# Splitting three of seven second-layer products into seven once more, in an attention and gated feed-forward kernel

## The chip, the cores and the metric

The kernel runs on one core of one Trainium2 chip. The metric is the device time in microseconds (us) of one execution; the figure for a kernel is the median of its runs. A profile of one execution goes with it: what each engine did and when. PE is the matrix engine (TensorE), PEld its weight loads, DVE is VectorE, ACT is ScalarE, POOL is GpSimd, SP the engine whose queue starts most DMAs.

## The reference

Everything is float32. For 8 batches of 576 rows, attention without a softmax, normalised by its root mean square, gives x of 4608 tokens by 512 features. Then comes a gated feed-forward layer with 1536 hidden features.

```python
kv  = einsum('bhsd,bhse->bhde', k, v)
out = einsum('bhsd,bhde->bhse', q, kv)
rms = sqrt(mean(out * out, axis=-1, keepdims=True) + 1e-06)
x   = (out / rms * g_norm).transpose(0, 2, 1, 3).reshape(4608, 512)

gate = 1.0 / (1.0 + exp(-(x @ w_gate)))
val  = x @ w_val
return gate * val @ w_out            # (4608, 512)
```

## The kernel before

The tokens are worked off in nine groups of 512. Group 0 is computed plainly. Groups 1 to 8 use Strassen's scheme in Winograd's form: a product of two 2x2 block matrices is made of seven block products instead of eight, at the price of sums of blocks before and after. The first layer (x with `w_gate` and `w_val`) uses it, and its own small part a second time within one of its products. The second layer (`h @ w_out`, h being gate times value) uses it once. Each product of the second layer is six matmuls, one for each 128 hidden features, of 128 tokens by 256 output columns. It is done for two halves g of the tokens:

```python
def second_layer_fast(c):
    b = {(j, n): w2[...] ...}                      # four blocks of w_out
    for g in range(2):
        t1, t2 = slice(P * g, P * g + P), slice(GH + P * g, GH + P * g + P)
        (i_a, pa), (i_b, pb) = (take() for _ in range(2))     # PSUM banks
        def product(ps, hs, ws, new):
            for f in range(NF2):                               # 6
                nc.tensor.matmul(ps, hs(f), ws[:, f, :], start=(new and f == 0), stop=(f == NF2 - 1), ...)
                if f % 3 == 2:
                    slot()                                     # one step of other work

        product(pa, lambda f: gv[c, f][:, t1], b[1, 1], True)
        o2 = sg_tile()
        nc.scalar.copy(out=o2[:, d1], in_=pa)
        product(pb, lambda f: s12[c, f][:, t2], t2w[2], True)
        o1 = sg_tile()
        tt(out=o1[:, d2], in0=pb, in1=o2[:, d1], op=ALU.add)
        product(pa, lambda f: gv[c, f + NF2][:, t1], b[2, 1], False)
        nc.scalar.copy(out=o1[:, d1], in_=pa)
        product(pb, lambda f: gv[c, f][:, t2], t2w[3], False)
        tt(out=o2[:, d2], in0=pb, in1=o2[:, d1], op=ALU.add)
        ...
            product(pc, lambda f: s12[c, f][:, t1], t2w[1][:, :, x], True)
            tt(out=o2x, in0=pc, in1=o2x, op=ALU.add)
        product(pb, lambda f: gv[c, f + NF2][:, t2], t2w[4], False)
        tt(out=o2[:, d1], in0=pb, in1=o2[:, d1], op=ALU.add)
        store(c, 2 + g, o2)
        ...
            product(pc, lambda f: s4[c, f][:, t1], b[2, 2][:, :, x], False)
            tt(out=o1[:, y], in0=pc, in1=o1[:, y], op=ALU.add)
        store(c, g, o1)
        if g == 1:
            load_late(c + 2)                                   # k and v two groups on
```

`tt` is VectorE's `tensor_tensor`. `s12` and `s4` are sums of h, made on VectorE at the end of each step of the first layer (`h_sum`, `h_sums`, lines 847 to 856). `t2w[1..4]` are sums of blocks of `w_out`, made once. In the very last half the two products marked with `x` are cut into two halves of 128 columns (`parts`), so that the last output can leave sooner.

The first layer needs sums of x and of its weights. Those of x are made on VectorE, in steps that are put in the queue `fill`, of which each call of `slot()` does one; those of the weights on GpSimd:

```python
def x_sums(c):                                      # 4 of 128x512 and, in x_sums2, 4 of 128x128
    sx[c] = s = sums.tile([P, 3, NK, GH], FP32, tag="sx", name="sx", bufs=1)
    return [lambda: tt(out=s[:, 0], in0=a[2, 1], in1=a[2, 2], op=ALU.add), ...] + x_sums2(c, a[1, 2])

def w_sum(f, i):                                    # 128x256, L720
    nc.gpsimd.tensor_tensor(out=tw[f, i], in0=..., in1=..., op=ALU.subtract)

def w_sums2(f):                                     # four of 128x128, L713
    nc.gpsimd.tensor_tensor(out=tw2[i], in0=in0, in1=..., op=ALU.subtract)

for c in range(1, NG):
    if c + 1 < B:
        steps = feed(c + 1)                         # attention of the next batch, as steps for slot()
        ...
        spread(steps, ...)
    first_layer_fast(c)                             # its last part starts the weight sums of the next group
    sums_of(c + 1)                                  # x_sums of the next group
    second_layer_fast(c)
    flush()
```

There are five PSUM banks for products; `take()` takes the one that has been free longest, `give()` puts it back. Every engine works through its instructions in the order of the program.

Of the kernel before, what the change touches and what calls it, by code (L numbers as in the profile page):

```python
# [20 lines left out]
def kernel(  # L21
# [313 lines left out]
    def slot():  # L335
        if fill:
            fill.popleft()()
# [3 lines left out]
    def feed(b):  # L341
# [34 lines left out]
        def two_pairs(n0):  # L376


            d = {}
            ms = sb.tile([P, NQ, NJ], FP32, tag="ms2", name="ms2", bufs=1)  # L380
            sq = sqs[:, 0:2 * S].rearrange("p (r c) -> p r c", r=NQ)
            units = [slice(NJ // 2 * i, NJ // 2 * (i + 1)) for i in range(2)]

            def by_head(t):
                return t.rearrange("p r (n d) -> p r n d", d=HD)

            def u_mm():
                d["u"] = u = at_ps()[:, 0:NQ, 0:2 * QC]
                for which in range(2):
                    for g in range(JH):  # L390
                        for i in range(NC):
                            for r in range(NQ):
                                for e in range(2):
                                    c, o = NJ * HD * e + QC * i + PH * g, HD * (JH * which + g)
                                    nc.tensor.matmul(u[HD * e:HD * e + HD, r, o:o + HD],  # L395
                                                     qTs[QB * r:QB * r + QB, (n0 + which) % 2, c:c + PH],
                                                     kvq[QB * r:QB * r + QB, (n0 + which) % NHP, NC * e + i],
                                                     start=(i == 0), stop=(i == NC - 1))

            def u_square():  # L400
                nc.scalar.activation(out=sq, in_=d["u"], func=AF.Square)

            def u_sum(i):
                nc.vector.tensor_reduce(out=ms[:, :, units[i]], in_=by_head(sq)[:, :, units[i]], axis=AX.X, op=ALU.add)

            def u_root():
                nc.scalar.activation(out=ms, in_=ms, func=AF.Sqrt, bias=eps, scale=1.0 / HD)

            def u_norm(i):
                if i == 0:  # L410
                    nc.vector.reciprocal(ms, ms)
                m_ = ms[:, :, units[i]]
                nc.vector.tensor_tensor(out=by_head(sq)[:, :, units[i]], in0=by_head(d["u"])[:, :, units[i]],
                                        in1=m_.unsqueeze(3).to_broadcast([P, NQ, NJ // 2, HD]), op=ALU.mult)

            def x_turn(i):


                for which in range(2):
                    nc.vector.transpose(xTs[:, i, which],  # L420
                                        sq.rearrange("p r (w g i c) -> p w i r g c", w=2, g=JH, i=NC)[:, which, i])
                m = n0 % NHP
# [426 lines left out]
    def h_sums(c, f):  # L849
# [5 lines left out]
        tt(out=one[:, h2], in0=one[:, h1], in1=one[:, h2], op=ALU.subtract)  # L855
        tt(out=s4[c, f], in0=two[:, h1], in1=s[:, h2], op=ALU.subtract)

    def second_layer_fast(c):
        b = {(j, n): w2[:, NF2 * (j - 1):NF2 * j, DH * (n - 1):DH * n] for j in (1, 2) for n in (1, 2)}
        d1, d2 = slice(0, DH), slice(DH, DM)  # L860
        for g in range(2):
            t1, t2 = slice(P * g, P * g + P), slice(GH + P * g, GH + P * g + P)
            (i_a, pa), (i_b, pb) = (take() for _ in range(2))

            last = (c, g) == (NG - 1, 1)
            parts = [slice(0, DH // 2), slice(DH // 2, DH)] if last else [slice(0, DH)]

            def product(ps, hs, ws, new):
                for f in range(NF2):
                    nc.tensor.matmul(ps, hs(f), ws[:, f, :], start=(new and f == 0), stop=(f == NF2 - 1),  # L870
                                     skip_group_check=True)
                    if f % 3 == 2:
                        slot()

            product(pa, lambda f: gv[c, f][:, t1], b[1, 1], True)
            o2 = sg_tile()
            nc.scalar.copy(out=o2[:, d1], in_=pa)
            product(pb, lambda f: s12[c, f][:, t2], t2w[2], True)
            o1 = sg_tile()
            tt(out=o1[:, d2], in0=pb, in1=o2[:, d1], op=ALU.add)  # L880
            product(pa, lambda f: gv[c, f + NF2][:, t1], b[2, 1], False)
            nc.scalar.copy(out=o1[:, d1], in_=pa)
            if last:
                store(c, g, o1, d1)
            product(pb, lambda f: gv[c, f][:, t2], t2w[3], False)
            tt(out=o2[:, d2], in0=pb, in1=o2[:, d1], op=ALU.add)
            pcs = []
            for x in parts:
                i_c, pc = take()
                pc = pc[:, 0:x.stop - x.start]  # L890
                pcs.append((i_c, pc))
                product(pc, lambda f: s12[c, f][:, t1], t2w[1][:, :, x], True)
                o2x = o2[:, DH + x.start:DH + x.stop]
                tt(out=o2x, in0=pc, in1=o2x, op=ALU.add)
            product(pb, lambda f: gv[c, f + NF2][:, t2], t2w[4], False)
            tt(out=o2[:, d1], in0=pb, in1=o2[:, d1], op=ALU.add)
            store(c, 2 + g, o2)
            give(i_a)
            give(i_b)
            for (i_c, pc), x in zip(pcs, parts):  # L900
                give(i_c)
                product(pc, lambda f: s4[c, f][:, t1], b[2, 2][:, :, x], False)
                y = slice(DH + x.start, DH + x.stop)
                tt(out=o1[:, y], in0=pc, in1=o1[:, y], op=ALU.add)
                if last:
                    store(c, g, o1, y, (nc.sync, nc.scalar))
            if not last:
                store(c, g, o1)
            if g == 1:
                load_late(c + 2)  # L910

    def sums_of(c):
        if c < NG:
            fill.append(lambda: fill.extendleft(reversed(x_sums(c))))

    sums = ctx.enter_context(tc.tile_pool(name="sums", bufs=2, side="right"))
    for n in (1, 2, 3, 4):
        for f in (0, NF2):
            w_sum(f, n)
# [27 lines left out]
    for c in range(1, NG):  # L947
        if c + 1 < B:
            steps = feed(c + 1)
            if c == 1:  # L950

                i = 4
                while w2_sums:
                    steps.insert(i, (DVE, w2_sums.popleft()))
                    i += 3
            spread(steps, (1, 2, 3, 4, 5) if c == 1 else (2, 3, 4, 5))
        first_layer_fast(c)
        sums_of(c + 1)
        second_layer_fast(c)
        flush()  # L960

# [29 lines left out]
```

## Time and profile before

| | |
|---|---|
| time, median of 3 runs | 1077.0 us (1076.07 to 1077.27) |
| span in the profile | 1073.9 us |
| mean granted TensorE clock | 0.998 |
| second layer of one group without attention steps (group 7) | 921.50 to 957.76 us |
| second layer of a group with attention steps (group 4) | 582.09 to 620.42 us |
| additions of L855 (VectorE, 128x256), min / median / max | 409 / 943 / 950 ns |
| additions of L702 (VectorE, 128x128), min / median / max | 281 / 281 / 699 ns |
| sums of L713 with two original blocks (GpSimd, 128x128), min / median / max | 445 / 459 / 933 ns |

How to read it: "busy" is the time in which an engine has at least one instruction running. The records of PE overlap, so its pace is read from the distance of start times and not from the duration of one. A line of the timeline has the start and the length in us, the engine, the line of the source, the operation, what is written and read, the shape, how many alike are merged (x12), and in brackets the idle time before it with what ended it. A matmul of float32 shows as two records.

### The profile page before, as it was taken

Reading aid. Unit: us, or ns where it says so; the run is one execution under the profiler, and the core shown is the slowest. Engines: PE = TensorE matmul, PEld = TensorE weight load, DVE = VectorE, ACT = ScalarE, POOL = GpSimd, SP = SyncE. Lnnn points to the kernel's source line nnn. Section 1 sums busy time; section 2 is a strip of 40 time slices with the busy share of each in tenths; the row PEclk is TensorE's granted clock in tenths of the full one; section 3 lists DMA queues with packets and bytes.
Section 4 is the critical chain, followed back from the end, with each engine's and each line's share of the span. In section 5 each row is a group of like instructions: output and inputs, shape, how many; then the busy total and the mean of one; then the engine's idle time right before and its main releaser. Section 6 shows DMA issues by size and latency. Waiting matters only on the chain.

```text
span 1073.9 us, 19464 instructions
## 1 busy us (share of the span) xinstructions
PE 1062.2 (99%) x7514; PEld 882.4 (82%) x7514; DVE 712.0 (66%) x1461; ACT 309.0 (29%) x737; POOL 442.1 (41%) x630
## 2 busy tenths in 40 slices
PE   8999999999999999999999999999999999999997
PEld 7544448888888888888888888888888888888886
DVE  4897767894579547863778357945786388628841
ACT  4654323331243113320433134312431122112210
POOL 0000035880367216640666046713663077307800
PEclk9999999999999999999999999999999999999999
DMA  9944710002400141012301140014001200010001
GB/s 259 254 157 157 244 29 22 24 17 60 119 12 13 45 128 36 12 35 62 100 23 34 42 120 13 25 45 137 13 12 27 58 2 1 2 38 1 1 1 40
DMA packets 69115, 64.96 MB, mean 60 GB/s; under 512 B 23712, under 2 KB 63008, under 8 KB 69024
## 3 DMA queue, kind: packets, MB, share of 16 engines
q1 hardware_dynamic: 68768, 63.69, 21.1%
q8 instruction: 60, 0.98, 0.4%
q14 instruction: 31, 0.25, 0.1%
q10 hardware_dynamic: 256, 0.03, 0.1%
HBM read 47.19 MB, written 9.44 MB: 53 GB/s over the span
## 4 chain that ended last, share of the span: by engine, by line
PE 97%; DVE 1%; DMA 1%; SPq 0%; issue 0%; ACT 0%; DVEq 0%
PE mm L728 46%; PE mm L870 27%; PE mm L732 7%; PE mm L556 7%; PE mm L653 4%; PE at L395 2%; PE at L354 1%; PE at L556 1%; DMA q<-in_q_dram 1%; PE two L291 0%; PE two L261 0%; PE mm L634 0%; PE two L318 0%; PE two L272 0%; PE at L360 0%; SPq L97 0%
## 5 line engine op out<-in xcount | busy, mean ns | idle before, releaser
L720 POOL TENSOR_TENSOR tw<-gv 128x256 f32<-128x256 f32 x192 | 156.2, 823 | 232.1 <-DVE w L202 145.0
L728 PE MATMUL mm<-xT,tw 128*128 128x256 f32 x768 | 198.4, 381 | 0.0
L728 PE MATMUL mm<-sx,tw 128*128 128x256 f32 x768 | 197.4, 380 | 0.0
L802 POOL TENSOR_TENSOR sg<-sg 128x256 f32<-128x256 f32 x48 | 35.6, 742 | 341.1 <-ACT sg L801 340.9
L720 POOL TENSOR_TENSOR tw<-gv,tw 128x256 f32<-128x256 f32 x192 | 155.0, 828 | 0.0
L728 PEld LDWEIGHTS mm<-xT,tw 128*128 128x128 f32 x768 | 137.3, 190 | 17.5 <-issue 2.9
L728 PEld LDWEIGHTS mm<-sx,tw 128*128 128x128 f32 x768 | 134.9, 191 | 12.4
L773 DVE TENSOR_TENSOR gv<-gv,sg 128x256 f32<-128x256 f32 x192 | 108.7, 585 | 0.0
L728 PE MATMUL mm<-sx,gv 128*128 128x256 f32 x384 | 91.2, 380 | 0.0
L728 PE MATMUL mm<-xT,gv 128*128 128x256 f32 x384 | 90.8, 379 | 0.0
L870 PE MATMUL mm<-w,gv 128*128 128x256 f32 x384 | 89.1, 381 | 0.7 <-DVE gv L773 0.7
L870 PE MATMUL mm<-t2w,gv 128*128 128x256 f32 x384 | 88.7, 381 | 0.0
L870 PE MATMUL mm<-w,s 128*128 128x256 f32 (+1 forms) x408 | 88.3, 367 | 0.0
L764 ACT ACTIVATE sg<-sg 128x256 f32<-128x256 f32 x96 | 40.0, 416 | 151.0 <-DVE sg L763 150.9
L739 ACT COPY sg<-mm 128x256 f32<-128x256 f32 x96 | 35.8, 373 | 162.7 <-PE mm L728 160.9
L870 PEld LDWEIGHTS mm<-w,gv 128*128 128x128 f32 x384 | 72.5, 190 | 12.2 <-DVE gv L773 2.5
L870 PEld LDWEIGHTS mm<-w,s 128*128 128x128 f32 x408 | 74.1, 190 | 9.4
L728 PEld LDWEIGHTS mm<-xT,gv 128*128 128x128 f32 x384 | 72.9, 190 | 10.4 <-issue 0.5
L728 PEld LDWEIGHTS mm<-sx,gv 128*128 128x128 f32 x384 | 72.5, 190 | 10.0
L870 PEld LDWEIGHTS mm<-t2w,gv 128*128 128x128 f32 x384 | 72.4, 190 | 10.0
L556 PE MATMUL mm<-xT,gv 128*128 128x512 f32 x176 | 77.4, 594 | 0.0
L745 DVE TENSOR_TENSOR gv<-mm,sg 128x256 f32<-128x256 f32 x96 | 37.0, 413 | 41.2 <-PE mm L728 37.8
(120 smaller groups left out, 1548.4 us busy)
## 6 DMA issues: line engine op xcount, KB each, us to landing
q<-in_q_dram SPq DMA_DIRECT2D x24, 288.0 KB
st<-in_moe_w_gate_dram SPq DMA_DIRECT2D x12, 512.0 KB
st<-in_moe_w_val_dram SPq DMA_DIRECT2D x12, 512.0 KB
st<-in_moe_w_out_dram SPq DMA_DIRECT2D x12, 512.0 KB
kv<-in_k_dram SPq DMA_DIRECT2D x24, 256.0 KB
kv<-in_v_dram SPq DMA_DIRECT2D x24, 256.0 KB
out_dram<-sg SPq DMA_DIRECT2D x23, 192.0 KB
xT<-xTs SPq DMA_DIRECT2D x48, 72.0 KB
```

What stands on the lines that cost most here:

```text
L395: nc.tensor.matmul(u[HD * e:HD * e + HD, r, o:o + HD], qTs[QB * r:QB * r + QB, (n0 + which) % 2, c:c + PH], kvq[QB * r:QB * r + QB, (n0 + ...
L556: nc.tensor.matmul(self.ps[i], w[("wg", "wv")[i], self.f][:, m, :], xT[self.c][:, m, :], start=(m == 0), stop=(m == NMT - 1), skip_group_c ...
L653: nc.tensor.matmul(ps[t], gv[0, f][:, P * t:P * t + P], w["wo", f], start=(f == 0), stop=(f == NFT - 1), skip_group_check=True)
L720: nc.gpsimd.tensor_tensor(out=tw[f, i], in0=b[in0], in1=b[in1] if isinstance(in1, tuple) else tw[f, in1], op=ALU.subtract)
L728: nc.tensor.matmul(ps, wt[:, m, :], xs[:, m, :], start=(new and m == 0), stop=(m == NK - 1), skip_group_check=True)
L732: nc.tensor.matmul(ps, wt, xs, start=new, stop=True, skip_group_check=True)
L739: nc.scalar.copy(out=d["sg"][:, h2], in_=d["pa"])
L745: tt(out=d["h"][:, h1], in0=d["pb"], in1=d["sg"][:, h2], op=ALU.add)
L764: nc.scalar.activation(out=d["sg"][:, h2], in_=d["sg"][:, h2], func=AF.Sigmoid)
L773: tt(out=d["h"][:, h], in0=d["h"][:, h], in1=d["sg"][:, h], op=ALU.mult)
L802: nc.gpsimd.tensor_tensor(out=g2[:, h1], in0=g2[:, h1], in1=g2[:, h2], op=ALU.add)
L870: nc.tensor.matmul(ps, hs(f), ws[:, f, :], start=(new and f == 0), stop=(f == NF2 - 1), skip_group_check=True)
```

## The change

Three of the seven products of the second layer, those with `b[2, 1]`, `t2w[4]` and `b[2, 2]`, are each taken over both halves of the tokens at once and split into seven smaller products by the same scheme: small products are three matmuls of 128 tokens by 128 columns. Seven times three matmuls of 128 columns stand in place of twice six matmuls of 256 columns. This is meant to take an eighth of these products' columns from the matrix engine.

Each split needs four sums of weights and four of h, each of three tiles of 128x128. There is no free memory for them, so they are written to places that are no longer read: the sums of x (`sx`, now one fixed tile), and columns of `gv` (h) and `s12` whose products are done. As these places are used again, the sums of weights are made anew in each group. The three sets of weight sums and one set of h sums are made on GpSimd, two sets of h sums on VectorE. The sums of x for the next group come only after split 1, which reads `sx`. Steps of the attention end earlier (idle steps removed, the sums of `w_out` placed at every second step instead of every third).

```diff
-        return steps + two_pairs(n0 + 2) + [(PE, idle)] * 4
+        return steps + two_pairs(n0 + 2)
...
-        sx[c] = s = sums.tile([P, 3, NK, GH], FP32, tag="sx", name="sx", bufs=1)
+        sx[c] = s = sx_tile
...
+    def sums2(engine, x, out, weights):             # 4 sums, each over N3 = 3 tiles
+        ...
+                engine.tensor_tensor(out=o[i][j], in0=u0, in1=u1, op=...)
...
     def second_layer_fast(c):
+        spare = sx[c].rearrange("p a k (h t) -> p (a k h) t", h=2)
+        a4, a2, a3 = h_quarters(gv, hi, 2), h_quarters(gv, hi, 0), h_quarters(s4, lo, 0)
+        b4, b2, b3 = (w_quarters(x) for x in (t2w[4], b[2, 1], b[2, 2]))
+        t4 = sums2(nc.gpsimd, b4, thirds([spare[:, i] for i in range(4 * N3)]), True)
+        for g in pair:
+            product(pa[g], of(gv, lo, g), b[1, 1], True)
+            nc.scalar.copy(out=o2[g][:, d1], in_=pa[g])
+        t2 = sums2(nc.gpsimd, b2, thirds(of(gv, lo, 0) + of(gv, lo, 1)), True)
+        for g in pair:
+            product(pb[g], of(s12, lo, 2 + g), t2w[2], True)
+            nc.scalar.copy(out=o1[g][:, d1], in_=o2[g][:, d1])
+            tt(out=o1[g][:, d2], in0=pb[g], in1=o2[g][:, d1], op=ALU.add)
+        r2 = thirds(of(s12, lo, 2) + of(s12, lo, 3))
+        s4_ = sums2(nc.gpsimd, a4, r2[:3], False)
+        for g in pair:
+            product(pb[g], of(gv, lo, 2 + g), t2w[3], False)
+            tt(out=o2[g][:, d1], in0=pb[g], in1=o2[g][:, d1], op=ALU.add)
+        t3 = sums2(nc.gpsimd, b3, thirds(of(gv, lo, 2) + of(gv, lo, 3)), True)
+        for g in pair:
+            product(pc, of(s12, lo, g), t2w[1], True)
+            tt(out=o2[g][:, d2], in0=pc, in1=o2[g][:, d1], op=ALU.add)
+            tt(out=o1[g][:, d2], in0=pc, in1=o1[g][:, d2], op=ALU.add)
+        s2_ = sums2(nc.vector, a2, thirds(of(s12, lo, 0) + of(s12, lo, 1))[:3], False)
+
+        def split(o, x, a, sa, w_, tw_, done=None):
+            ...                                     # small(): 3 matmuls of 128 columns
+            small(pd, a[1, 1], w_[1, 1], True)
+            add(o[0][:, l], pd)
+            small(pf, a[1, 2], w_[2, 1], True)
+            add(o[0][:, l], pf)
+            slot()
+            small(pd, sa[2], tw_[2], False)         # goes on in the bank that add read
+            add(o[0][:, r], pd)
+            small(pe, sa[1], tw_[1], True)
+            add(o[1][:, r], pe)
+            slot()
+            small(pd, sa[3], tw_[3], False)
+            tt(out=y, in0=y, in1=pd.unsqueeze(1).to_broadcast([P, 2, P]), op=ALU.add)
+            small(ph, a[2, 2], tw_[4], True)
+            add(o[1][:, l], ph)
+            slot()
+            small(pe, sa[4], w_[2, 2], False)
+            add(o[0][:, r], pe)
+            slot()
+
+        split(o2, d1, a4, s4_, b4, t4)
+        for g in pair:
+            store(c, 2 + g, o2[g])
+        if not ends:
+            fill.extend(x_sums(c + 1))
+        s3_ = sums2(nc.vector, a3, r2[:3], False)
+        split(o1, d1, a2, s2_, b2, t2)
+        ...
+            split(o1, d2, a3, s3_, b3, t3)
+            for g in pair:
+                store(c, g, o1[g])
+        load_late(c + 2)
...
-                    i += 3
+                    i += 2
...
-        sums_of(c + 1)
```

More of the change, by code (lines that the diff above doesn't have):

```diff
@@ L856, in h_sums @@
         tt(out=s4[c, f], in0=two[:, h1], in1=s[:, h2], op=ALU.subtract)
+    N3 = NF2 // 2
+    d1, d2 = slice(0, DH), slice(DH, DM)
+    tok = [slice(P * i, P * i + P) for i in range(G // P)]
+    def sums2(engine, x, out, weights):
+        o = dict(zip((1, 2, 4, 3), out))
+        if weights:
+            ops = ((1, (1, 2), (1, 1)), (2, (2, 2), 1), (4, (2, 1), 2), (3, (2, 2), (1, 2)))
+        else:
+            o[3] = x[2, 1]
+            ops = ((1, (2, 1), (2, 2)), (2, 1, (1, 1)), (3, (1, 1), (2, 1)), (4, (1, 2), 2))
+        for i, in0, in1 in ops:
+            for j in range(N3):
+                u0, u1 = (x[n][j] if isinstance(n, tuple) else o[n][j] for n in (in0, in1))
+                engine.tensor_tensor(out=o[i][j], in0=u0, in1=u1,
+                                     op=ALU.add if i == 1 and not weights else ALU.subtract)
+        return o
@@ L858, in second_layer_fast @@
     def second_layer_fast(c):
         b = {(j, n): w2[:, NF2 * (j - 1):NF2 * j, DH * (n - 1):DH * n] for j in (1, 2) for n in (1, 2)}
[L860 to L870, printed above, removed]
-                                     skip_group_check=True)
[L872 to L910, printed above, removed]
@@ L912, in sums_of, with product @@
-    def sums_of(c):
-        if c < NG:
-            fill.append(lambda: fill.extendleft(reversed(x_sums(c))))
+        ends = c == NG - 1
+        pair = range(2)
+        lo, hi = range(NF2), range(NF2, NFT)
+        def product(ps, hs, ws, new):
+            for f in range(NF2):
+                nc.tensor.matmul(ps, hs[f], ws[:, f, :], start=(new and f == 0), stop=(f == NF2 - 1),
+                                 skip_group_check=True)
+                if f % N3 == N3 - 1:
+                    slot()
@@ new lines, in of, with thirds, h_quarters, w_quarters @@
+        def of(tiles, fs, t):
+            return [tiles[c, f][:, tok[t]] for f in fs]
+        def thirds(tiles):
+            return [tiles[i:i + N3] for i in range(0, len(tiles), N3)]
+        def h_quarters(tiles, fs, t):
+            return {(i, k): of(tiles, fs[N3 * (k - 1):N3 * k], t + i - 1) for i in (1, 2) for k in (1, 2)}
+        def w_quarters(ws):
+            return {(k, n): [ws[:, f, tok[n - 1]] for f in range(N3 * (k - 1), N3 * k)] for k in (1, 2) for n in (1, 2)}
+        spare = sx[c].rearrange("p a k (h t) -> p (a k h) t", h=2)
@@ new lines, in second_layer_fast @@
+        a4, a2, a3 = h_quarters(gv, hi, 2), h_quarters(gv, hi, 0), h_quarters(s4, lo, 0)
+        b4, b2, b3 = (w_quarters(x) for x in (t2w[4], b[2, 1], b[2, 2]))
+        t4 = sums2(nc.gpsimd, b4, thirds([spare[:, i] for i in range(4 * N3)]), True)
+        o2, o1, pa, pb = {}, {}, {}, {}
+        for g in pair:
+            i_, pa[g] = take()
+            product(pa[g], of(gv, lo, g), b[1, 1], True)
+            o2[g] = sg_tile()
+            nc.scalar.copy(out=o2[g][:, d1], in_=pa[g])
+            give(i_)
@@ new lines, in second_layer_fast @@
+        t2 = sums2(nc.gpsimd, b2, thirds(of(gv, lo, 0) + of(gv, lo, 1)), True)
+        i_b = {}
+        for g in pair:
+            i_b[g], pb[g] = take()
+            product(pb[g], of(s12, lo, 2 + g), t2w[2], True)
+            o1[g] = sg_tile()
+            nc.scalar.copy(out=o1[g][:, d1], in_=o2[g][:, d1])
[5 more added lines that the diff above has]
+            tt(out=o2[g][:, d1], in0=pb[g], in1=o2[g][:, d1], op=ALU.add)
+            give(i_b[g])
@@ new lines, in second_layer_fast, with small, add @@
+        t3 = sums2(nc.gpsimd, b3, thirds(of(gv, lo, 2) + of(gv, lo, 3)), True)
+        for g in pair:
+            i_, pc = take()
+            product(pc, of(s12, lo, g), t2w[1], True)
+            tt(out=o2[g][:, d2], in0=pc, in1=o2[g][:, d1], op=ALU.add)
+            tt(out=o1[g][:, d2], in0=pc, in1=o1[g][:, d2], op=ALU.add)
+            give(i_)
+        s2_ = sums2(nc.vector, a2, thirds(of(s12, lo, 0) + of(s12, lo, 1))[:3], False)
+        def split(o, x, a, sa, w_, tw_, done=None):
+            (i_d, pd), (i_e, pe), (i_f, pf), (i_h, ph) = (take() for _ in range(4))
+            pd, pe, pf, ph = (ps[:, 0:P] for ps in (pd, pe, pf, ph))
+            l, r = slice(x.start, x.start + P), slice(x.start + P, x.stop)
+            def small(ps, hs, ws, new):
+                for j in range(N3):
+                    nc.tensor.matmul(ps, hs[j], ws[j], start=(new and j == 0), stop=(j == N3 - 1),
+                                     skip_group_check=True)
+            def add(t, ps):
+                tt(out=t, in0=ps, in1=t, op=ALU.add)
+            small(pd, a[1, 1], w_[1, 1], True)
[9 more added lines that the diff above has]
+            small(pd, sa[3], tw_[3], False)
+            y = o[1][:, x].rearrange("p (n c) -> p n c", n=2)
+            tt(out=y, in0=y, in1=pd.unsqueeze(1).to_broadcast([P, 2, P]), op=ALU.add)
+            small(ph, a[2, 2], tw_[4], True)
+            add(o[1][:, l], ph)
+            slot()
+            if done:
+                done()
+            small(pe, sa[4], w_[2, 2], False)
+            add(o[0][:, r], pe)
+            slot()
+            for i in (i_d, i_f, i_h, i_e):
+                give(i)
@@ new lines, in second_layer_fast @@
+        split(o2, d1, a4, s4_, b4, t4)
[5 more added lines that the diff above has]
+        split(o1, d1, a2, s2_, b2, t2)
+        if ends:
+            for g in pair:
+                store(c, g, o1[g], d1)
+            l, r = slice(DH, DH + P), slice(DH + P, DM)
+            split(o1, d2, a3, s3_, b3, t3,
+                  lambda: [store(c, 1, o1[1], d2), store(c, 0, o1[0], l)])
+            store(c, 0, o1[0], r, (nc.sync, nc.scalar))
+        else:
+            split(o1, d2, a3, s3_, b3, t3)
+            for g in pair:
+                store(c, g, o1[g])
@@ L916 @@
+        load_late(c + 2)
     sums = ctx.enter_context(tc.tile_pool(name="sums", bufs=2, side="right"))
+    sx_tile = sums.tile([P, 3, NK, GH], FP32, name="sx", bufs=1)
     for n in (1, 2, 3, 4):
```

## The prediction

> **What bounds the kernel now.** I read the page's first lines, then the chain that ended last, then the matrix engine's order of time in one second layer.
>
> ```profile
> span 1073.9 us, 19464 instructions
> ...
> PE 1062.2 (99%) x7514; PEld 882.4 (82%) x7514; DVE 712.0 (66%) x1461; ACT 309.0 (29%) x737; POOL 442.1 (41%) x630
> ...
> PE 97%; DVE 1%; DMA 1%; SPq 0%; issue 0%; ACT 0%; DVEq 0%
> PE mm L728 46%; PE mm L870 27%; PE mm L732 7%; PE mm L556 7%; PE mm L653 4%; PE at L395 2%; PE at L354 1%; PE at L556 1%; DMA q<-in_q_dram 1%; PE two L291 0%; PE two L261 0%; PE mm L634 0%; PE two L318 0%; PE two L272 0%; PE at L360 0%; SPq L97 0%
> ```
>
> TensorE (PE) is busy for 99% and is 97% of the chain, so the kernel gains only if PE has less to stream, and loses whatever makes PE wait. The second layer (L870) is 27%. What a product costs there is read from start times, since neighbouring records overlap. This is the timeline of PE in the last group, where the old kernel already has two products cut into 128-column halves:
>
> ```profile
> 1055.20 2.75 PE L870 MATMUL mm<-t2w,gv 128*128 128x256 f32 x12
> 1057.79 2.84 PE L870 MATMUL mm<-w,s 128*128 128x128 f32 x24
> 1060.47 2.75 PE L870 MATMUL mm<-t2w,gv 128*128 128x256 f32 x12
> 1063.06 2.84 PE L870 MATMUL mm<-w,s 128*128 128x128 f32 x24
> ```
>
> Each fp32 matmul is two records. A product of six matmuls (x12) takes 1057.79 - 1055.20 = 2.59 us, 0.216 us a record of 256 columns. The 24 records of 128 columns take 1060.47 - 1057.79 = 2.68 us, 0.112 us each. So a half-width matmul is nearly half as dear, even with weights of its own each time.
>
> The other two engines matter because the change gives them its additions. First VectorE (DVE) in the group that starts its second layer at 921.50, then the same lines in the last group:
>
> ```profile
> 923.64 0.94 DVE L854 TENSOR_TENSOR s<-s,gv 128x256 f32<-128x256 f32 x1
> 924.51 0.94 DVE L855 TENSOR_TENSOR gv<-gv 128x256 f32<-128x256 f32 x1
> 925.38 0.94 DVE L856 TENSOR_TENSOR s<-gv,s 128x256 f32<-128x256 f32 x1
> ...
> 929.41 0.29 DVE L702 TENSOR_TENSOR sx<-sx,xT 128x128 f32<-128x128 f32 x1
> 929.62 0.28 DVE L703 TENSOR_TENSOR xT<-xT 128x128 f32<-128x128 f32 x1
> ...
> 1030.77 0.42 DVE L854 TENSOR_TENSOR s<-s,gv 128x256 f32<-128x256 f32 x1
> 1031.11 0.42 DVE L855 TENSOR_TENSOR gv<-gv 128x256 f32<-128x256 f32 x1
> ```
>
> and GpSimd (POOL) beside the first of them and after:
>
> ```profile
> 924.27 1.77 POOL L720 TENSOR_TENSOR tw<-gv,tw 128x256 f32<-128x256 f32 x2
> 963.04 0.73 POOL L802 TENSOR_TENSOR sg<-sg 128x256 f32<-128x256 f32 x1 [37.00 <-ACT sg L801]
> ...
> 968.31 0.46 POOL L713 TENSOR_TENSOR tx<-gv,gv 128x128 f32<-128x128 f32 x1
> ```
>
> A 256-column addition with both inputs in SBUF starts every 0.34 us on DVE when POOL is idle (1030.77 to 1031.11) and every 0.87 us when POOL works (923.64 to 924.51). A 128-column one starts every 0.21 us alone (929.41 to 929.62). POOL is idle from 926.0 to 963.0, the whole second layer but its first 4.5 us.
>
> **What the skill says.** The Trainium skill, "SBUF — State Buffer", section "Who interferes with whom": a VectorE instruction with two SBUF inputs contends with a GpSimd instruction that reads SBUF. The trace agrees: 0.34 us against 0.87 us above. "PSUM — Partial Sum Buffer", section "Engine vs sequencer instructions": ScalarE, VectorE and GpSimd queues are strict FIFO; an addition at the head of DVE's queue therefore holds back a later one that PE needs. The trace shows every engine in program order. "TensorE: Matmul & The Clock Gate", section "Step-by-step: what each phase is for": LDWEIGHTS are pulled ahead of running matmuls. It agrees: a weight load lasts 190 ns, yet 128-column records start every 112 ns. The same page, section "What's actually happening": after an idle window of about 3.4 us PE's clock is halved until it has been busy for about as long. No run here shows it; the granted clock was 0.998.
>
> **The change, part by part.** The second layer had 14 products per group of 512 tokens (seven for each half), 14 x 2.59 = 36.3 us. Now three of the seven, taken over both halves, are done by a further seven-product scheme ("split").
>
> Gain on PE: a split has 7 small products of 3 matmuls of 128 columns, 21 x 2 x 0.112 = 4.70 us, and replaces two products, 5.18 us. That is 0.48 per split, 1.45 us per group, and 11.6 us for eight groups. The two halved products of the last group cost 0.09 each too much before, 0.2 us in all. So the most that can come of it is 12 us, 1.1%.
>
> Additions: per group 48 new ones of 128 x 128 on POOL (three sets of weights, one set of h sums, 12 each) and 24 on DVE (two sets of h sums), besides seven PSUM additions per split. POOL's pace is its 0.46 us less the 0.04 us by which its neighbours overlap, 0.42 us, so a set is 5.0 us and four are 20.2 us. This fits POOL's idle time. The sets on DVE are a different matter, because of where they stand. In the built order the first set (s2) follows the last plain product, and the first PSUM addition of split 1 follows that set. Yet PE's third small product accumulates into the bank that this addition must read first: it waits for DVE.
>
> Times from the start of a second layer (without the attention work, which shifts PE by about 1.75 us in groups 1 to 6):
> - Eight plain products end at 8 x 2.59 = 20.7. PE goes on with two small products to 22.1 and then needs the addition.
> - DVE sees the last product at 20.9 (0.16 for the drain, 2.75 - 2.59), does its two additions at 0.35 each, and starts s2 at 21.6.
> - POOL starts at 4.5 and ends its sets at 9.5, 14.6, 19.6 and, alone, 24.7. At 21.6 it still has some 7 operations of the last one. From 256 columns, a contended pair takes 0.87 where alone they take 0.34 + 0.69; in that proportion a pair of 128 columns takes 0.85 x (0.21 + 0.42) = 0.53 us. I take 0.55. Seven pairs end at 25.5, and the five left on DVE at 26.5.
> - The addition for PE is done at about 26.8. PE has waited 26.8 - 22.1 = **4.7 us**. In groups 1 to 6 PE comes 1.75 later, but so does POOL by about 1 (it shares with DVE's attention work): I take 4.6 for all seven.
> - In split 2 it happens again: the second set (s3) overwrites places that split 1 reads, so it starts after split 1's last addition, 0.4 after PE's end, and takes 12 x 0.21 = 2.5, now with POOL idle, plus 0.3 for the addition. PE has 2 x 0.67 = 1.34 of its own work meanwhile: 3.2 - 1.3 = **1.9 us** of waiting.
> - The eight sums of the next x stand between additions of splits 2 and 3 (four of 0.6 to 0.7, four of 0.2 to 0.3). Followed through by hand they cost PE about 0.35.
> - Output is stored later, and the next loads of k and v stand behind it on the same DMA queue. The old kernel has them just in time for L354, so I add 0.5 in five groups, 2.5 in all.
>
> Sum for groups 1 to 7: 4.6 + 1.9 + 0.35 - 1.45 = +5.4, times 7 = +37.8. The last group has no next weights on POOL, so POOL is done by 20.2 and s2 runs uncontended: 12 x 0.21 = 2.5 instead of 4.9, a wait of about 2.4; 2.4 + 1.9 - 1.45 - 0.2 = +2.7. With the 2.5 of the loads: +43. **1077 + 43 = 1120 us.**
>
> The removed idle steps and the denser placing (every second place instead of third) only make the attention steps end earlier, so that x sums can follow; they take nothing from PE.
>
> **Rivals.** (a) *The waits are hidden and PE's saving stands*: 1065 us. For it: DVE is 66% busy on average and waits for PE through most of the old second layer. Against it: the 24 DVE operations are not spread over that slack but stand in two blocks directly ahead of additions that PE waits for, while a split's PE work is only 4.7 us. (b) *No contention between POOL and DVE at 128 columns*, or POOL is done earlier: then the first wait is 2.4 in all groups, +43 - 7 x 2.2 = +28, 1105 us. For it: no 128-column pair is in the trace. Against it: the 256-column pairs. (c) *The long waits also slow PE's clock*: waits of 4.7 us are longer than the window, so some would be followed by 3.4 us at half rate. An estimate from that page is up to 1.7 us each, at most 8 x 1.7 = 14 us, 1134 us. (d) *POOL becomes the bound*: its h sums for split 1 end at 19.6, and are needed at 22.1. If its pace were 0.55 rather than 0.42, they would end at 4.5 + 36 x 0.55 = 24.3, still ahead of DVE's release at 26.8; but its last set would then keep contending for longer, and the first wait would grow by about 2 us, to 1134 us.
>
> **Range and chances.** The centre is 1120; (b) gives the lower side, (c) and (d) the upper. The limits are set a little outside (b) and (c): 1102 to 1138. Within 2% means below 1098.5, which needs half of the two waits to be absent: 0.11. Faster by over 2% would need more than PE's whole saving: 0.01. Slower by over 2%: 0.88.
>
> **What would show it.** Right: PE's busy time falls, but its idle time before the small products on DVE's additions is about 6 to 7 us per group; in split 1 the gap before the third small product is 4 to 5 us, in split 2 about 2, in split 3 below 0.5; small records start every 0.112 us; the 128-column DVE additions of s2 last over 0.4 us beside POOL and those of s3 0.28. Wrong: gaps below 1 us before the third small product, or s2 finished while the plain products still run; small records well above 0.112 us, which would make PE itself dearer; or gaps that name POOL or a DMA.

## The result, and the profile after

The changed kernel takes 1120.3 us (median of 4 runs, 1118.4 to 1127.2), the kernel before 1076.5 us (1076.0 to 1077.3). The ratio is 1.042, with a 95% interval of 1.037 to 1.047: the change makes the kernel 4% slower.

First the page of the changed kernel, the same lines as those shown of the kernel before:

```profile
span 1116.6 us, 21273 instructions
...
PE 1065.5 (95%) x7922; PEld 895.3 (80%) x7922; DVE 801.2 (72%) x1803; ACT 307.6 (28%) x737; POOL 603.1 (54%) x1014
...
PE 93%; DVE 5%; DMA 1%; issue 0%; ACT 0%; POOL 0%; POOLq 0%
PE mm L728 45%; PE mm L888 15%; PE mm L949 9%; PE mm L732 7%; PE mm L556 7%; PE mm L653 4%; DVE s L876 4%; PE at L395 2%; PE at L354 1%; PE mm L634 1%; PE at L556 1%; DVE sg L953 1%; DMA kv<-in_v_dram 1%; PE two L261 1%; PE two L291 1%; DVE gv L876 0%
```

The span grew by 42.7 us while PE's share fell from 99% to 95%: PE now stands idle for some 51 us instead of 12. In the chain, 5% is VectorE, 4% of it the new additions of h (`s`, L876) and 1% the PSUM addition behind them (L953). In the changed kernel L888 is a plain product of the second layer, L949 a matmul of a split.

The view of waits (engine and line, what it waited for, us in total, times, the longest) puts a number on it:

```profile
PE mm L949 <- DVE sg L953: 39.7, 17, 5.1
```

Two of these per group stand in the timeline of PE, here group 7, which has no attention steps:

```profile
972.94 1.50 PE L949 MATMUL mm<-t2w,gv 128*128 128x128 f32 x12
979.53 2.90 PE L949 MATMUL mm<-sx,s 128*128 128x128 f32 x12 [5.08 <-DVE sg L953]
982.22 2.20 PE L949 MATMUL mm<-sx,gv 128*128 128x128 f32 x12
...
988.09 1.60 PE L949 MATMUL mm<-gv,s 128*128 128x128 f32 x12 [1.66 <-DVE sg L953]
```

The brackets are the two waits: 5.08 us ahead of the third small product of split 1, 1.66 us ahead of that of split 2. The second line shows something else too: the 12 records after the first wait last 2.90 us, those after the second wait 1.60. That is a further loss, which no bracket shows. Group 4, which has attention steps:

```profile
627.21 1.58 PE L949 MATMUL mm<-sx,s 128*128 128x128 f32 x12 [3.13 <-DVE sg L953]
628.63 1.55 PE L949 MATMUL mm<-sx,gv 128*128 128x128 f32 x12
...
633.85 1.60 PE L949 MATMUL mm<-gv,s 128*128 128x128 f32 x12 [1.67 <-DVE sg L953]
```

Its first wait is only 3.13 us, and there is no slow stretch behind it. The first waits are 3.05 to 3.14 us in groups 1 to 6, 5.08 in group 7 and 2.23 in group 8. The second waits are 1.66 to 1.67 in all.

Why does group 7 wait 5 us? Its timelines of VectorE,

```profile
973.82 3.55 DVE L876 TENSOR_TENSOR s<-gv 128x128 f32<-128x128 f32 x3
977.28 0.68 DVE L876 TENSOR_TENSOR s<-s,gv 128x128 f32<-128x128 f32 x3
...
979.10 0.67 DVE L953 TENSOR_TENSOR sg<-mm,sg 128x128 f32<-128x128 f32 x2
```

and of GpSimd:

```profile
975.52 1.29 POOL L876 TENSOR_TENSOR gv<-w 128x128 f32<-128x128 f32 x3
```

Three additions of VectorE take 3.55 us in the first line and 0.68 in the next. The instructions of that source line have a median of 279 ns and a longest of 3144 ns: it is one addition that is held, from 973.82 until GpSimd's last set ends at 975.52 + 1.29 = 976.81. GpSimd is not slowed: three operations in 1.29 us, as when alone. Group 4 shows the same, on VectorE

```profile
623.45 1.60 DVE L876 TENSOR_TENSOR s<-gv 128x128 f32<-128x128 f32 x3
```

and on GpSimd:

```profile
623.21 1.29 POOL L876 TENSOR_TENSOR gv<-w 128x128 f32<-128x128 f32 x3
```

GpSimd ends at 624.50, so the first addition is held for about 1 us only. Counted from the start of the second layer GpSimd ends at nearly the same time in both groups (group 4: 624.50 - 599.78 = 24.7; group 7: 976.81 - 952.22 = 24.6), but in group 4 the attention work makes PE and VectorE come 2.1 us later.

Last, the slow stretches. A view of two stretches, behind the first wait of group 4 and of group 7 (columns: the stretch, its length, busy time and instructions of PE, PEld, DVE, ACT and POOL, then PEclk, the DMA share, GB/s):

```profile
627.20:630.70 3.50, 3.49 (x31) 3.50 (x32) 1.56 (x5) 0.00 (x0) 0.00 (x0) 1.00 0.10 26
979.50:984.30 4.80, 4.77 (x25) 4.80 (x26) 1.28 (x4) 0.00 (x0) 0.00 (x0) 0.57 0.00 0
```

PE is busy without a break in both, yet it gets 31 records into 3.5 us at a clock of 1.00 and only 25 into 4.8 us at 0.57. A loss can be taken from start times: from the start of the `mm<-sx,s` records to the start of `mm<-t2w,s`, 24 records on, is 630.01 - 627.21 = 2.80 us in group 4, and what another group has above 2.80 is lost to the clock. In the profiled run groups 3, 7 and 8 lose 2.45, 1.92 and 1.58 us, the others nothing. Group 3 loses 0.4 more after this stretch, which makes 6.3 us in all. I call this the half-rate loss below.

### The profile page after: what moved, and what is told of

It reads as the page before. It is cut to its first block, busy times and chain, and to the rows that moved or that the text cites. A ratio compares the mean times of both kernels' runs of the same rounds, so it can differ in the third digit from the quotient of the medians.

```text
span 1116.6 us, 21273 instructions
## 1 busy us (share of the span) xinstructions
PE 1065.5 (95%) x7922; PEld 895.3 (80%) x7922; DVE 801.2 (72%) x1803; ACT 307.6 (28%) x737; POOL 603.1 (54%) x1014
## 4 chain that ended last, share of the span: by engine, by line
PE 93%; DVE 5%; DMA 1%; issue 0%; ACT 0%; POOL 0%; POOLq 0%
PE mm L728 45%; PE mm L888 15%; PE mm L949 9%; PE mm L732 7%; PE mm L556 7%; PE mm L653 4%; DVE s L876 4%; PE at L395 2%; PE at L354 1%; PE mm L634 1%; PE at L556 1%; DVE sg L953 1%; DMA kv<-in_v_dram 1%; PE two L261 1%; PE two L291 1%; DVE gv L876 0%
## 5 line engine op out<-in xcount | busy, mean ns | idle before, releaser
L773 DVE TENSOR_TENSOR gv<-gv,sg 128x256 f32<-128x256 f32 x192 | 111.1, 598 | 0.0
L728 PEld LDWEIGHTS mm<-xT,gv 128*128 128x128 f32 x384 | 72.3, 190 | 10.0 <-issue 0.5
L953 DVE TENSOR_TENSOR sg<-mm,sg 128x128 f32<-128x128 f32 x144 | 41.7, 290 | 37.6 <-PE mm L949 33.8
L745 DVE TENSOR_TENSOR gv<-mm,sg 128x256 f32<-128x256 f32 x96 | 37.1, 413 | 40.4 <-PE mm L728 37.1
L763 DVE TENSOR_TENSOR sg<-mm,sg 128x256 f32<-128x256 f32 x96 | 40.7, 424 | 30.8 <-PE mm L728 30.5
L556 PEld LDWEIGHTS mm<-xT,gv 128*128 128x128 f32 x176 | 32.6, 190 | 37.4 <-issue 35.9
L749 DVE TENSOR_TENSOR gv<-mm,gv 128x256 f32<-128x256 f32 x96 | 40.4, 420 | 29.3 <-PE mm L728 28.2
L713 POOL TENSOR_TENSOR tx<-gv,tx 128x128 f32<-128x128 f32 x96 | 53.2, 555 | 7.5
L749 DVE TENSOR_TENSOR gv<-mm,sg 128x256 f32<-128x256 f32 x96 | 40.1, 417 | 14.3 <-PE mm L728 11.9
```

Source lines behind the costliest of these rows:

```text
L556: nc.tensor.matmul(self.ps[i], w[("wg", "wv")[i], self.f][:, m, :], xT[self.c][:, m, :], start=(m == 0), stop=(m == NMT - 1), skip_group_c ...
L713: nc.gpsimd.tensor_tensor(out=tw2[i], in0=in0, in1=tw2[in1] if isinstance(in1, int) else in1, op=ALU.subtract)
L728: nc.tensor.matmul(ps, wt[:, m, :], xs[:, m, :], start=(new and m == 0), stop=(m == NK - 1), skip_group_check=True)
L749: tt(out=d["h"][:, h2], in0=ps, in1=d.pop("u")[:, h2], op=ALU.add)
L773: tt(out=d["h"][:, h], in0=d["h"][:, h], in1=d["sg"][:, h], op=ALU.mult)
L953: tt(out=t, in0=ps, in1=t, op=ALU.add)
```

## The experiments

The theory after this reading: the loss is made of wait 1 (on s2, held by GpSimd), wait 2 (on s3, uncontended), and a half-rate loss behind wait 1. PE's own work is what it was meant to be. The rival readings: that the split itself, with its smaller matmuls, is dearer on PE; that the delay is VectorE's own amount of work; and that the half rate has a cause of its own. All diffs are against the changed kernel.

**1. Both sets of h sums on VectorE left out.** The output then lacks what they would contribute; PE's matmuls are all there.

```diff
     def sums2(engine, x, out, weights):
+        if engine is None:
+            return o
-        s2_ = sums2(nc.vector, a2, ...)
+        s2_ = sums2(None, a2, ...)
-        s3_ = sums2(nc.vector, a3, r2[:3], False)
+        s3_ = sums2(None, a3, r2[:3], False)
```

> Leaves out the 24 VectorE additions per group that make the h sums s2 and s3 (their places are read unsummed); everything else stays. Theory (the two blocks on VectorE stand ahead of additions that TensorE waits for): the waits of 3.3 to 5.3 us in split 1 and 1.8 us in split 2 go, and with them the slow clock; what stays is TensorE's saving less some small waits from the sums of x: 1077 - 12 + 3 to 5 = 1068 to 1070 us. Rival (the back and forth between TensorE and VectorE within a split, or the later loads of k and v, cost the time): little changes, above 1105 us.

Measured: 1073.6 us (1071.8 to 1076.3), ratio to the kernel before 0.997 (0.996 to 0.998). The splits' waits on VectorE are gone, and the granted clock stays at 1.00 until PE has done its work. So 47 us of the changed kernel's time hang on 24 additions per group, and the splits themselves are not dear. The result lies 3 to 4 us above what was expected. Its second layers take 37.39 us in groups with attention steps, 0.95 below the old 38.34 and not the 1.45 of the product count; and the first layers after groups 3 and 4 are 2.7 and 0.7 us longer than before. PE waits 1.6 us once on the load of v (L354).

**2. Only s2 left out** (s3 is done; the output lacks the part of s2).

> Leaves out only s2 (12 VectorE additions per group, ahead of split 1). Theory: the wait of split 1 goes (3.3 us in six groups, 5.3 in the seventh, 2.4 in the last, 27 in all) and the 5 to 10 us of slow clock that follow it; split 2 keeps its 1.8 us. 1120 - 27 - 5 to 10 = 1083 to 1088 us. Rival (one long VectorE queue: what is saved ahead of split 1 is waited for later): above 1100 us.

Measured: 1084.3 us (1083.6 to 1086.2), ratio 1.007 (1.004 to 1.010). Wait 2 stays at 1.66 us in every group, wait 1 and the half rate are gone. The profiled spans differ by 1116.6 - 1082.7 = 33.9 us. Taken by start times (some 0.2 above the brackets) wait 1 is 6 x 3.3 + 5.25 + 2.4 = 27.5 us; together with the half-rate loss of 6.3 that gives 33.8. The sum of the two terms is thereby confirmed.

**3. Only s3 left out** (s2 is done; the output lacks the part of s3).

> Leaves out only s3 (12 VectorE additions per group, between splits 1 and 2). Theory: 8 x 1.8 = 15 us less, 1103 to 1107 us, and the two savings of e2 and e3 add up to that of e1 within 4 us. Rival: sums of x move up and take the place of the wait, above 1112 us.

Measured: 1111.4 us (1110.7 to 1111.6), ratio 1.032 (1.029 to 1.034): slower than expected. Wait 2 is gone in all groups. But behind the unchanged first wait the clock is now slow in seven groups instead of three. Group 4 in the timeline of PE:

```profile
621.53 2.90 PE L951 MATMUL mm<-sx,s 128*128 128x128 f32 x12 [3.12 <-DVE sg L955]
624.23 1.76 PE L951 MATMUL mm<-sx,gv 128*128 128x128 f32 x12
```

The same wait as in the changed kernel (3.13), now followed by 12 records in 2.70 us. The half-rate loss adds up to 10.4 us against 6.3. So the length of a wait alone doesn't decide whether the clock drops (what does is shown below, under "The clock"); and leaving out s3 saved 9.0 us of the median, though the second waits that it removed make 8 x 1.83 = 14.6.

**4. GpSimd's last set left out**, which s2 runs into (`t3`; the output lacks its part). All of VectorE's work stays.

```diff
-        t3 = sums2(nc.gpsimd, b3, ...)
+        t3 = sums2(None, b3, ...)
```

> Leaves out the third set of weight sums on GpSimd (12 operations per group, those that still run when VectorE starts s2); VectorE's work stays. Theory, as the trace of the changed kernel shows the first addition of s2 held until GpSimd stops: the wait of split 1 falls to the uncontended 2.4 us in every group (0.9 less in six, 2.9 less in one: 8 us) and, being short, costs less slow clock (up to 8 us): 1104 to 1112 us. Rival (the additions are slow for another reason, and GpSimd does not matter): 1118 to 1122 us.

Measured: 1114.8 us (1110.1 to 1115.8), ratio 1.034 (1.031 to 1.038). On VectorE the first three additions of s2 now take as long as the others,

```profile
620.37 0.68 DVE L878 TENSOR_TENSOR s<-gv 128x128 f32<-128x128 f32 x3
```

and PE's first wait falls to 2.22 us in every group, group 7 included:

```profile
623.21 2.23 PE L951 MATMUL mm<-sx,s 128*128 128x128 f32 x12 [2.22 <-DVE sg L955]
625.24 2.52 PE L951 MATMUL mm<-sx,gv 128*128 128x128 f32 x12
```

So GpSimd held the addition: this is shown. What is left, 2.22, is VectorE's own 12 additions. The time fell by less than expected for the reason seen in the last two lines: after 2.22 us of waiting the 24 records take 4.38 us instead of 2.80. Seven groups lose 1.5 to 1.6 us this way, 10.9 in all. Working it out: waits shorter by 6 x 0.92 + 2.86 = 8.4, half-rate loss larger by 10.9 - 6.3 = 4.6, net -3.8; the spans differ by 1112.1 - 1116.6 = -4.5.

**5. Wait 1 filled with matmuls that nobody reads** (ten, into an empty bank), to see whether it is the idle time that slows the clock. The computation is unchanged.

```diff
             add(o[0][:, l], pf)
             slot()
+            if o is o2:
+                for _ in range(10):
+                    nc.tensor.matmul(bank(free[0])[:, 0:P], a[1, 1][0], w_[1, 1][0], start=True, stop=True, ...)
```

> Adds ten matmuls of 128 columns that nobody reads, into a free bank, where TensorE waits in split 1 (10 x 2 x 0.112 = 2.2 us of work within a wait of 2.4 to 5.3 us). If the slow clock after the wait comes from TensorE standing idle, the records after it take 0.112 us again in most groups, and in spite of 8 x 2.2 = 18 us more work the time falls by 4 to 8 us, to 1112 to 1116 us, with less scatter between runs. Rival (the slow records have another cause): 1118 to 1124 us, or up to 18 us more if the added work is not hidden in the wait.

Measured: 1125.6 us (1124.9 to 1130.4), ratio 1.047 (1.045 to 1.049). The size was missed, the point was not. PE's timeline in group 4:

```profile
626.38 5.31 PE L962 MATMUL mm<-t2w,gv 128*128 128x128 f32 x20
631.52 1.50 PE L949 MATMUL mm<-sx,s 128*128 128x128 f32 x12
```

The 20 filling records needed 631.52 - 626.38 = 5.14 us, 0.257 each instead of the 0.112 I counted on, so they overfilled the wait by about 1.8 us. But behind them the clock is 1.00 (mean of the whole run 0.999, against 0.991) in every group. The half rate comes from PE standing idle. The sum fits: the wait is overfilled by 6 x 1.84 = 11.0 us in groups 1 to 6 and by 2.7 in group 8, and cut by 0.1 in group 7; less the half-rate loss of 6.3 that makes +7.3, and the spans differ by 1123.7 - 1116.6 = 7.1.

**6. The same with four** filling matmuls.

> As the fill with ten matmuls, but with four: in that run a filling record started every 0.257 us, not every 0.112, so ten overfilled the wait by 1.8 us per group. Four take 8 x 0.257 = 2.1 us, less than the shortest wait of 2.4. If standing idle is what slows the clock, the small records after the wait take 0.112 us in nearly all groups and the time falls to 1111 to 1116 us. Rival (the slow records come from the small matmuls or from something else): 1118 to 1124 us.

Measured: 1116.8 us (1116.0 to 1117.7), ratio 1.037 (1.036 to 1.039), some 3.5 us below the changed kernel, where 4 to 9 had been expected. A rest of the wait is left (1.28 us in group 4). Behind wait 1 groups 2 and 7 still lose 1.5 and 2.3 us to the clock, the other six nothing. A third stretch at half rate, from 541.25 to 544.66, stands in a first layer, behind a wait of 1.57 us on the load of v.

**7. Both sets early on VectorE, GpSimd paused meanwhile.** s2 and s3 are written to other places that are free earlier (columns of `gv`, and old columns of x), so that they need not stand right before the additions that PE waits for. GpSimd waits for s3 at a one-column operation (`gate`) before its other two weight sets. The computation is unchanged.

```diff
-        t2 = sums2(nc.gpsimd, b2, ...)            # both moved
-        t3 = sums2(nc.gpsimd, b3, ...)
+        s2_ = sums2(nc.vector, a2, thirds(of(gv, lo, 0) + of(gv, lo, 1))[:3], False)
         ...
+            if g == 0:                             # between the last two plain products
+                s3_ = sums2(nc.vector, a3, thirds(spare_x[:9]), False)
+        nc.gpsimd.tensor_tensor(out=gate, in0=s3_[4][2][:, 0:1], in1=s3_[4][2][:, 0:1], op=ALU.add)
+        t2 = sums2(nc.gpsimd, b2, thirds(of(s12, lo, 0) + of(s12, lo, 1)), True)
+        t3 = sums2(nc.gpsimd, b3, thirds(of(gv, lo, 2) + of(gv, lo, 3)), True)
```

> The same computation in another order: s2 and s3 are written to places free earlier (columns of gv after two products, the old x of the group), so VectorE makes them during the plain products, in a pause of GpSimd; the weight sums t2 and t3 follow only after s3, and the sums of x after split 2. Theory: no long wait is left, the group's second layer takes 34.8 us and 0.3 to 1 more, 8 x 0.5 to 1.2 us less than before, less 2 us for the loads: 1067 to 1074 us, faster than both kernels. Rival (a split cannot be fed by VectorE in time): waits inside the splits stay, above 1085 us.

Measured: 1088.6 us (1087.4 to 1090.2), ratio 1.012 (1.010 to 1.013). Much better than the changed kernel, but not what was expected. On VectorE in group 4:

```profile
606.72 2.50 DVE L876 TENSOR_TENSOR gv<-gv 128x128 f32<-128x128 f32 x12
609.14 1.55 DVE L420 STREAM_TRANSPOSE xTs<-sqs 128x288 f32<-128x288 f32 x4
610.61 0.38 DVE L936 TENSOR_TENSOR sg<-mm,sg 128x256 f32<-128x256 f32 x1
```

s2 takes 2.50 us, uncontended, but VectorE is now full from 606.72 on with s2, the transposes of the attention and s3, so the PSUM additions that PE waits for are late by the same queue: 1.9 us of wait in groups 1 to 6, and 0.5 in groups 7 and 8, which have no attention steps. In groups 1 and 4 the clock is halved behind it, 1.6 us each. "Earlier" was not early enough.

**8. Both sets as early, without the pause of GpSimd.** s2 now goes to old columns of x, s3 to old columns of x and of `s12`, as GpSimd's sets keep the places and the order of the changed kernel. The sums of x stay behind split 1.

> As the order with early s2 and s3, but GpSimd keeps the order of the changed kernel and so works without a pause from 4.5 to 24.4 us of each second layer. If VectorE and GpSimd take turns (0.53 us for a pair, as I assumed), s2 and s3 cost 12 us of VectorE time between 16 and 28: about 5 us of wait per group, 1100 to 1110 us. If GpSimd keeps VectorE out until it stops, VectorE gets through s2, s3 only after 24.4 us: at 24.4 + 24 x 0.21 + 1.7 = 31 against 22.1 wanted (1.75 less with attention work), 7 to 9 us of wait per group, 1125 to 1150 us.

Measured: 1149.3 us (1148.2 to 1150.6), ratio 1.068 (1.067 to 1.070). PE waits 8.2 to 8.8 us in groups 1 to 7. VectorE, group 7,

```profile
997.28 8.93 DVE L876 TENSOR_TENSOR xT<-gv 128x128 f32<-128x128 f32 x3
```

GpSimd's last set,

```profile
1004.39 1.27 POOL L876 TENSOR_TENSOR gv<-w 128x128 f32<-128x128 f32 x3
```

and PE:

```profile
1012.13 2.90 PE L952 MATMUL mm<-sx,s 128*128 128x128 f32 x12 [8.77 <-DVE sg L956]
```

One addition of 128 columns, which takes 0.28 us by itself, lasts 8.5 us (the longest of its line is 8528 ns): until GpSimd's stream of back-to-back operations is over at 1005.66. Between these two streams nothing was shared in turns, as in the second picture of the expectation. This is the sharpest of the runs: the longer GpSimd's stream still lasts, the longer one single addition is held.

**9. s2 handed to GpSimd, s3 first on VectorE.** s3 comes at the very start of the second layer, before GpSimd's sets (it waits at `gate`); GpSimd then does the first weight set, the two sets of h sums that splits 1 and 2 need, and the other two weight sets. The x sums come before split 3. The computation is unchanged.

```diff
+        s3_ = sums2(nc.vector, a3, thirds(spare_x[:9]), False)
+        nc.gpsimd.tensor_tensor(out=gate, in0=s3_[4][2][:, 0:1], in1=s3_[4][2][:, 0:1], op=ALU.add)
         t4 = sums2(nc.gpsimd, b4, ...)
         ...
+        s2_ = sums2(nc.gpsimd, a2, thirds(of(gv, lo, 0) + of(gv, lo, 1))[:3], False)
+        t2 = sums2(nc.gpsimd, b2, thirds(of(s12, lo, 0) + of(s12, lo, 1)), True)
+        t3 = sums2(nc.gpsimd, b3, thirds(of(gv, lo, 2) + of(gv, lo, 3)), True)
```

> The same computation. s3 is made first of all, on VectorE, in places of the group's old x, before GpSimd starts its sets (GpSimd waits for it with a one-column addition); s2 goes to GpSimd, between the h sums of split 1 and the weight sums t2. So VectorE has no addition with two inputs in SBUF left while GpSimd works, until the sums of x in split 3. By the measured pace of 0.413 us GpSimd ends t4, s4, s2, t2, t3 at about 12, 17, 22, 27 and 32 us of the second layer, each ahead of its split (20.7, 25.4 and 30.1, and their third small products 1.3 later). Theory: no wait above 0.5 us in the splits, no slow clock, the time of the kernel that leaves s2 and s3 out, 1070 to 1075 us. Rival (a split itself costs, or GpSimd becomes the bound): above 1079 us.

Measured: 1073.2 us (1072.5 to 1074.1), ratio 0.9965 (0.9953 to 0.9978). This is 0.3% faster than the kernel before and 47 us faster than the changed kernel, with the same matmuls and the same additions in another order and on other engines. PE, group 4:

```profile
604.38 1.50 PE L953 MATMUL mm<-t2w,gv 128*128 128x128 f32 x12
605.72 1.54 PE L953 MATMUL mm<-sx,s 128*128 128x128 f32 x12
607.10 1.54 PE L953 MATMUL mm<-sx,gv 128*128 128x128 f32 x12
```

and GpSimd, where s2 now is:

```profile
599.26 5.00 POOL L876 TENSOR_TENSOR gv<-gv 128x128 f32<-128x128 f32 x12
```

The split runs through without a wait or a half-rate stretch. s2 takes 5.0 us on GpSimd instead of 2.5 on VectorE, and costs nothing there, as it is done before PE needs it. A second layer with attention steps takes 37.11 us against 38.34 before. Over eight groups these 1.23 us would make 9.8; only 2.7 arrive in the span (1073.9 to 1071.2). The other 7.1 stand outside the second layers: the first layers of groups 3, 4, 5 and 8 are 0.6, 2.4, 1.2 and 0.9 us longer than before, and from the start of PE's last record to the end of the span it takes 10.3 us instead of 8.3. In the first layers the waits on the load of v (L354, 1.7 us in all) and on ScalarE (L791, 1.6 us in all) are new against the old kernel; why the end is longer was not tried.

## Why the prediction was right in its number, and where a step was not

The terms over eight groups, from the profiled run, beside what the prediction had (us):

| term | predicted | measured |
|---|---|---|
| PE's saving | -11.8 | about -10 (split 4.77 instead of 4.70) |
| wait 1, groups 1 to 6 | 6 x 4.6 = 27.6 | 6 x 3.3 = 19.8 |
| wait 1, group 7 | 4.6 | 5.25 |
| wait 1, group 8 | 2.4 | 2.4 |
| wait 2 | 8 x 1.9 = 15.2 | 8 x 1.83 = 14.6 |
| small losses in the splits | 7 x 0.35 = 2.5 | about 2: 42.55 - 38.34 in group 4, less the terms above, is 0.3 |
| loads of k and v | 2.5 | 2.6 in the first layers of groups 4 and 5, 1.55 of it a wait of L354 |
| half-rate loss | 0 | 6.3 |

PE's saving is from experiment 9's timeline: 42 records of a split start between 604.38 and 609.15, 4.77 us, in place of 5.18; 8 x 3 x 0.41 = 9.8, and 0.2 for the old halved products. The measured terms make 43.0; the span grew by 42.7. That the total fits to 0.3 us is partly luck: wait 1 came out 7 us too large and the half rate, put at zero, took its place.

**PE's saving**: right. Small records start every 0.112 us with weights of their own each time; the split itself took 0.07 more than reckoned.

**Where s2 and s3 stand, and who waits for them**: right. Both waits are where they were said to be, on the additions named, and experiments 1 to 3 show that 47 us go when the two sets go. The second wait's size was right too, as nothing contends with it.

**Contention in wait 1**: the failed step. The prediction let the two engines take turns, "in that proportion a pair of 128 columns takes 0.85 x (0.21 + 0.42) = 0.53 us. I take 0.55. Seven pairs end at 25.5". Instead GpSimd went on at its own pace and ended at 24.6, the 24.7 that the prediction had for it alone; VectorE's first addition was held all that while, and the other eleven ran in 0.28 each. For group 7 both pictures lead to nearly the same release (27.2 against 26.8), hence 5.25 and not 4.7. They part in groups 1 to 6. "PE comes 1.75 later, but so does POOL by about 1 (it shares with DVE's attention work)" was wrong: GpSimd doesn't give way and ends at 24.7 as well, so the 2.1 us by which PE comes later come off the wait: 5.25 - 2.1 = 3.2, and 3.3 was measured. The predicted sign, "the 128-column DVE additions of s2 last over 0.4 us", accordingly failed: their median is 279 ns and one of a set lasts up to 3144. So did the 6 to 7 us of idle time per group: in group 4 the two waits are 3.13 + 1.67 = 4.8 us. The trace of before had no pair of two 128-column operations, and 256-column operations that alternate were taken as a model for it.

The section "Who interferes with whom" of the Trainium skill, "SBUF — State Buffer", says that the shared pair of ports is an exclusive lock and that issue order decides who blocks. The measurements agree with an exclusive lock, but the addition is held for a whole stream of operations (3.1 us, 8.5 us), not for the one that was first.

**The clock**: rival (c) was half right. The half rate does follow the waits, and experiment 5 shows that filling the wait removes it; but it appears in three groups of eight and costs 6.3 us, where (c) allowed for up to 14. The reason given with it failed: "waits of 4.7 us are longer than the window". The section "What's actually happening" of the Trainium skill, "TensorE: Matmul & The Clock Gate", gives a window of about 3.4 us that runs freely, and the prediction noted that no run showed the halving. These runs do, and the window with it. In every profile the times at which the granted clock changes lie whole multiples of 3.41 us apart: in the changed kernel half rate lasts from 502.39 to 509.22, from 976.85 to 983.67 and from 1092.90 to 1096.31. What counts is how much of a wait falls into one such window. Here are two windows around the first wait of group 3 (3.14 us) and two around that of group 4 (3.13 us), columns as above:

```profile
498.98:502.39 3.41, 1.05 (x10) 0.86 (x8) 3.41 (x13) 0.00 (x0) 1.47 (x4) 1.00 0.28 65
502.39:505.81 3.42, 2.64 (x12) 2.67 (x13) 1.21 (x6) 0.00 (x0) 0.00 (x0) 0.50 0.18 46
621.86:625.27 3.41, 2.22 (x17) 1.92 (x15) 2.49 (x7) 0.00 (x0) 2.64 (x7) 1.00 0.29 73
625.27:628.68 3.41, 1.47 (x13) 1.50 (x14) 2.38 (x11) 0.00 (x0) 0.00 (x0) 1.00 0.26 65
```

In group 3 PE idles 3.41 - 1.05 = 2.36 us of the first window, and the next is at half rate. In group 4 the wait is split into 1.19 and 1.94 us, and the clock stays. In the nine profiles without filling matmuls, up to PE's last matmul, every window at full rate with 2.05 us or more of idle time is followed by half rate, and none with 1.87 or less; in between lie two of 1.90 that are and one of 1.94 that isn't. This also answers experiments 3 and 4. In experiment 3 the same wait of group 4 lies almost whole in one window (2.94 us of idle time from 617.94 to 621.35). In experiment 4 at least 2.05 of the 2.22 us lie in one window in seven groups, and in the eighth they are split into 0.86 and 1.36. In experiment 6 windows with 1.3 to 1.6 us of idle time were enough in three places; why is open.

**Rival (a)**, hidden waits, is refuted by the brackets. **Rival (b)**, no contention: refuted by experiment 4, which takes GpSimd's last set away and shortens wait 1 to 2.2 us. **Rival (d)**, GpSimd as the bound: refuted by its pace of 0.41 us, and no wait of PE in a second layer names it.

**PE's busy time** was to fall as a sign. It rose, from 1062.2 to 1065.5: a record at half rate is twice as long and counts as busy. In experiments 1 and 2, without half-rate stretches, it is 1056.2 and 1056.8.

## What to carry to other kernels

When work moves to an engine with idle time, look at which instruction of that engine stands next in line for the busy one: 24 short additions per group cost 47 us because they stood right before an addition that the matrix engine waited for, and cost it no wait once half of them stood on an engine half as fast and the others in an earlier place. A 128x128 addition on VectorE with both inputs in SBUF, next to an unbroken stream of such operations on GpSimd, should be reckoned as starting when that stream ends; for other shapes look for the pair in a trace. And a wait of 2 to 5 us on PE can cost another 1.3 to 2.9 us through the clock behind it, so that shortening a wait, as experiment 4 did, can bring less than its length.

## What the runs showed of the hardware that was not expected

- A 128x128 fp32 addition of VectorE with both inputs in SBUF lasted up to 3.14 and, in experiment 8, 8.53 us beside back-to-back 128x128 additions of GpSimd (one every 0.41 us), which were not slowed. VectorE's 128x256 additions with one input in PSUM kept their 0.42 us beside the same stream. In the first layer of the same kernel 128x256 additions of both engines alternate, 0.87 us each. GpSimd's 128x128 stream doesn't always win either: as it began in group 1 of the changed kernel, a 128x256 addition of VectorE (L856, 242.12 to 242.79) came in between two of its operations, and the second of these took 0.64 us instead of 0.46. Why one starves and the other takes turns stays open; it was not tried.
- PE's granted clock changed only at whole multiples of 3.41 us and went to half after a window of that length in which PE had idled 2.05 us or more. While PE still had work, half rate lasted 3.41, 6.83 or 10.24 us; it cost 1.3 to 2.9 us behind one wait. Waits of 3.13 and 3.14 us did and didn't bring it, by where they fell.
- Matmuls that each start anew in the same PSUM bank with the same operands started every 0.257 us a record, where records of the splits take 0.112.
